# Sums of logarithms as two single-pass products of split parts, in a gated linear attention followed by a feed-forward network

## The chip, the cores and the metric

The kernel runs on one core of a Trainium2 chip. The metric is the device time of one execution in microseconds; the median of four runs of the kernel before is 568.94 us (568.49 to 570.35). Traces come from one further look at such an execution, the one of 568.91 us.

## What is computed

Attention first: for each of 4 batches and 8 heads a 48 x 48 state is decayed by alpha, step by step over 768 positions, and read by q. Its output, one row of 384 numbers for each of 3072 tokens, goes through a feed-forward network with 2048 hidden units.

```python
for t in range(S):                      # S = 768, alpha between 0.8 and 1
    state = alpha[:, :, t, :, None] * state + np.einsum('bhd,bhe->bhde', k[:, :, t], v[:, :, t])
    y[:, :, t] = np.einsum('bhd,bhde->bhe', q[:, :, t], state)
x = y.transpose(0, 2, 1, 3).reshape(B * S, H * D)     # 3072 x 384
h = np.maximum(x @ w_in, 0.0)                         # w_in 384 x 2048, stored as 64-bit floats
out = (h * h @ w_out).astype(np.float32)              # w_out 2048 x 384, likewise
```

## The kernel before

**Blocks.** The sequence is cut into 6 chunks of 128 positions; a block is one chunk of one batch, all heads, 24 blocks in all. Block n is chunk n // 4 of batch n % 4. Within a block the recurrence is solved with cumulated decays: the logarithm of alpha is summed over the positions from the block's start (a product with a triangle of ones), q is multiplied by the exponential of that sum and k by the exponential of its negative; then scores, masked, times v, plus q times the state that came in.

The steps of a block that matter here, with the lines of the profile:
- `ln` (243): ScalarE takes the logarithm of alpha's tile in place, 128 positions x 384 columns.
- `cs` (248): TensorE multiplies it with `causal`, the 128 x 128 triangle of ones, in fp32, into one PSUM bank.
- `eb`, `ei` (258, 262): ScalarE takes exp of the sums and of their negative into the tiles `b` and `inv`, of which there are two each.
- `mq`, `mk` (266): VectorE multiplies q and k by them.
- `bl`, `br` (279, 285): SP's DMAs copy the last row of `b` to DRAM and back, turned, into one of four small tiles `last`, by which the state is multiplied (450).
- `turn` (515) and its copies (523): q and k are transposed on TensorE and copied out by ScalarE.
- `scores` (404), `state_sums` (430), `masked` (414), `y` (380), `ev` (538): the rest, in functions `ga` and `gb` that handle two blocks at a time.

**Feed-forward.** Four blocks make a group of 512 tokens, six groups in all. Group 0 is multiplied plainly (621, 696). For groups 1 to 5 both matrix products are done with seven instead of eight half-size products, the sums and differences of halves being made by VectorE (`combine`, line 570): a stage of products with `w_in` (659, results combined on 672 to 679) and then a stage of 28 units with `w_out` (730; results combined on 748 to 766). One unit is four fp32 products of 192 columns.

**Order.** Nothing is scheduled by a tool: each engine runs its instructions in the order in which the program issues them. Attention for group g + 1 is laid between the units of group g's last stage. Every pair of blocks has a table `PLAN` of times in units at which its steps are issued, counted from the pair's start; `weave` issues a step before the first unit whose time has come. The pairs that start with blocks 8, 14, 18 and 22 start at time 0 of a stage, those of 10 and 12 at units 7 and 14 of the first such stage, those of 16 and 20 at unit 13.5 of theirs. The pair's first lines before the change:

```python
PLAN = (
    (0, "ln0"),
    (0.5, "ln1"),
    (2.0, "cs0 eb0 ei0"),
    (3.0, "cs1 eb1 ei1"),
    (3.5, "mk0"),
```

So in a stage the logarithms are issued before units 0 and 1, and the two products with the triangle before units 2 and 3. Each `cs` is followed on SP's queue by the load of alpha for the block after next, into the tile that is read by `cs`. Blocks 0 to 3 are issued from a list written by hand; blocks 4 to 7 are laid between the units of group 0.

Of the kernel before, what the change touches and what calls it, by code (L numbers as in the profile page):

```python
# [7 lines left out]

FP32 = mybir.dt.float32
U32 = mybir.dt.uint32  # L10
AF = mybir.ActivationFunctionType
ALU = mybir.AluOpType
# [3 lines left out]
GB = 4  # L16
# [7 lines left out]
def kernel(  # L24
# [25 lines left out]
    nc = tc.nc  # L50
    B, H, S, D = q.shape
    C = 128
    NCH = S // C
    NP = H // 2
# [8 lines left out]
    consts = ctx.enter_context(tc.tile_pool(name="consts", bufs=1))  # L63
# [3 lines left out]
    p2 = ctx.enter_context(tc.tile_pool(name="p2", bufs=2))  # L67
# [6 lines left out]
    def kept(name, n, shape):  # L74
        return [consts.tile(shape, FP32, name=f"{name}{i}") for i in range(n)]

    s_t = [p2.tile([128, NP, 64], FP32, tag="s", name="s", bufs=B + 2) for _ in range(B)]
    for t in s_t:
# [9 lines left out]
    NW = 8  # L88
    w_in = [consts.tile([128, KM, DF // NW], FP32, name=f"w_in{i}") for i in range(NW)]
    w_out = [consts.tile([128, NJ // NW, DM], FP32, name=f"w_out{i}") for i in range(NW)]  # L90
    HM, NR2 = DM // 2, NJ // 4
    tsum = [kept(f"t{i}_", NR2, [128, 2, HM]) for i in (1, 2, 4)]

    def flat(t):
        return t.rearrange("a x y -> a (x y)")
# [4 lines left out]
    for x, n, i in (("q", 2, 6), ("q", 3, 7), ("k", 3, 5)):  # L100
        t = lent[x, n] = flat(w_out[i])[:, 0 : 64 * H].rearrange("a (h d) -> a h d", h=H)
# [19 lines left out]
    def load_weights(i):  # L121
        dst = (w_in + w_out)[i]
        dt = moe_w_in.dtype
        raw = dst if dt == FP32 else raw_pool.tile(list(dst.shape), dt, tag="raw", name="raw")
        raws[i] = raw
# [13 lines left out]
    def convert_first(i):  # L139
        if moe_w_in.dtype == FP32:  # L140
            return
        w = (w_in + w_out)[i].rearrange("a k f -> a (k f)")
        n = w.shape[1]
        words = raws.pop(i).rearrange("a k f -> a (k f)").bitcast(U32)
        words = words.rearrange("a (n h) -> a n h", h=2)
        lo, hi = words[:, :, 0], words[:, :, 1]
        power = cv_pool.tile([128, n], U32, tag="power", name="power")
        upper = cv_pool.tile([128, n], U32, tag="upper", name="upper")
        nc.vector.tensor_scalar(
            out=power, in0=hi, scalar1=20, scalar2=0x7FF,  # L150
            op0=ALU.logical_shift_right, op1=ALU.bitwise_and,
        )
        nc.vector.tensor_scalar(
            out=upper, in0=hi, scalar1=0xFFFFF, scalar2=None, op0=ALU.bitwise_and
        )
        half[i] = w, lo, hi, power, upper
# [46 lines left out]
    make_identity(nc, ident)  # L203
    causal = consts.tile([128, C], FP32, name="causal")
    make_upper_triangular(nc, causal, 1.0, diag=True)
    halves_mask = consts.tile([128, C // 2], FP32, name="halves_mask")
    for i in range(2):
        rows = slice(64 * i, 64 * (i + 1))
        nc.gpsimd.tensor_copy(out=halves_mask[rows], in_=causal[rows, rows])
    last_t = kept("last", 4, [128, NP])  # L210
    for t in last_t:
        nc.gpsimd.memset(t, 0.0)
    dram = ctx.enter_context(tc.tile_pool(name="dram", bufs=1, space=bass.MemoryType.DRAM))
    rows_t = [dram.tile([1, H * D], FP32, name=f"row{n}") for n in range(NBLK)]
    rebias = consts.tile([128, 1], FP32, name="rebias")
# [13 lines left out]
    blk = [{} for _ in range(NBLK)]  # L229
    xT = {}  # L230

    def bank(n, name, shape=(NP, C)):

        if n < GB and name in ("sc", "y"):
            return ps_ffn.tile([128, *shape], FP32, tag="f", name=name)
        return ps_att.tile([128, *shape], FP32, tag="att", name=name)
# [4 lines left out]
    def ln(n):  # L241
        la = blk[n]["la"] = tile_of("a", n)
        nc.scalar.activation(out=la, in_=la, func=AF.Ln)

    def cs(n):

        ps = blk[n]["cs"] = bank(n, "cs")
        nc.tensor.matmul(  # L248
            out=ps.rearrange("a p t -> a (p t)")[:, 0 : H * D], lhsT=causal,
            rhs=blk[n].pop("la"), start=True, stop=True,  # L250
        )

    def sums_of_logs(n):
        return blk[n]["cs"].rearrange("a p t -> a (p t)")[:, 0 : H * D]
# [83 lines left out]
    def am(n):  # L338

        ps = blk[n].pop("sc")  # L340
        for e in range(2):
            nc.vector.copy_predicated(
                out=am_t[n % NAM][:, e],
                mask=causal.bitcast(U32).unsqueeze(1).to_broadcast([128, NP, C]), data=ps[e],
            )
# [63 lines left out]
    def masked(n):  # L409
# [3 lines left out]
        for e in range(2):  # L413
            nc.vector.copy_predicated(  # L414
                out=am_h(n)[:, e, n % 2], data=ps[e][:, 0],
                mask=halves_mask.bitcast(U32).unsqueeze(1).to_broadcast([128, NP, 64]),
            )

    def am_h(n):
        t = am_t[n // 2 % NAM].rearrange("a e p t -> a (e p t)")  # L420
        return t.rearrange("a (e m p t) -> a e m p t", e=2, m=2, p=NP)
# [351 lines left out]

    stages = [(ln, cs, eb, ei, mq, mk, bl, br), (qT, qc, kT, kc), (sc, am), (kv, y, ev, st)]
    steps = {f.__name__: f for stage in stages for f in stage}
    steps["load"] = load
    steps["weights"] = lambda _: load_weights(to_load.pop(0))
# [15 lines left out]
    for word in first.split():  # L795
# [6 lines left out]

    PLAN = (
        (0, "ln0"),
        (0.5, "ln1"),
        (2.0, "cs0 eb0 ei0"),
        (3.0, "cs1 eb1 ei1"),
        (3.5, "mk0"),
# [62 lines left out]
    for g in range(1, NG):  # L871
# [8 lines left out]
        if g + 1 < NG:  # L880
            n = GB * (g + 1) + 2
# [35 lines left out]
```

## Time and profile before

| what | value |
|---|---|
| median of 4 runs | 568.94 us |
| the profiled execution | 568.91 us, of which its span (first to last instruction) is 566.9 us |
| TensorE busy, multiplying | 553.7 us, 98% of the span |
| TensorE busy, loading weights (beside it) | 470.4 us, 83% |
| VectorE busy | 327.0 us, 58%, in 655 instructions |
| ScalarE busy | 223.7 us, 39% |
| GpSimd busy | 5.8 us, 1% |
| line 248, the product with the triangle | 48 instructions (two for each of 24 blocks), 486 to 590 ns each as recorded |
| granted TensorE clock | 1.000 over the span |

The profile lists instructions by engine: PE is TensorE's multiplying, PEld its loading of weights, DVE VectorE, ACT ScalarE, POOL GpSimd, SPq the queue from which SP issues DMAs. "L248" is line 248 of the kernel. Instructions on TensorE overlap, so that the length of one is more than what it adds to the stream; what it adds is seen from the start of one to the start of the next. In timeline rows the columns are the start in us, the length, the engine, the line, the operation, the tile written and the tiles read, the shapes, the count that was merged into the row and, in brackets, how long the engine had been idle and what ended that.

### The profile page before, as it was taken

Reading aid. Unit: us, or ns where it says so; the run is one execution under the profiler, and the core shown is the slowest. Engines: PE = TensorE matmul, PEld = TensorE weight load, DVE = VectorE, ACT = ScalarE, POOL = GpSimd, SP = SyncE. Lnnn points to the kernel's source line nnn. Section 1 sums busy time; section 2 is a strip of 40 time slices with the busy share of each in tenths; the row PEclk is TensorE's granted clock in tenths of the full one; section 3 lists DMA queues with packets and bytes.
Section 4 is the critical chain, followed back from the end, with each engine's and each line's share of the span. In section 5 each row is a group of like instructions: output and inputs, shape, how many; then the busy total and the mean of one; then the engine's idle time right before and its main releaser. Section 6 shows DMA issues by size and latency. Waiting matters only on the chain.

```text
span 566.9 us, 12556 instructions
## 1 busy us (share of the span) xinstructions
PE 553.7 (98%) x5306; PEld 470.4 (83%) x5306; DVE 327.0 (58%) x655; ACT 223.7 (39%) x533; POOL 5.8 (1%) x28
## 2 busy tenths in 40 slices
PE   8889999999999999999899999999999999999997
PEld 6654455668889899888899988999988999988996
DVE  4988688685874745565562566462466551466430
ACT  5469865442334353234143333433333340333100
POOL 2010000000000000000000000000000000000000
PEclk9999999999999999999999999999999999999999
DMA  9978576401003645000333200333300000100001
GB/s 164 254 177 217 152 183 209 114 1 57 1 1 57 114 98 103 28 0 16 57 72 77 65 1 1 57 59 71 86 0 2 0 3 1 57 0 2 1 0 57
DMA packets 117087, 37.04 MB, mean 65 GB/s; under 512 B 108820, under 2 KB 111912, under 8 KB 117032
## 3 DMA queue, kind: packets, MB, share of 16 engines
q1 hardware_dynamic: 117032, 36.25, 28.4%
q8 instruction: 42, 0.69, 0.5%
q14 instruction: 13, 0.11, 0.1%
HBM read 31.49 MB, written 4.75 MB: 64 GB/s over the span
## 4 chain that ended last, share of the span: by engine, by line
PE 95%; DMA 2%; DVE 2%; issue 1%; SPq 0%; ACT 0%; DVEq 0%
PE h L659 34%; PE o L730 33%; PE o L696 7%; PE h L621 7%; PE y L380 4%; PE cs L248 3%; PE T L515 2%; PE sckv L404 2%; PE sckv L430 2%; DMA raw<-in_moe_w_in_dram 1%; DMA k_in<-in_k_dram 1%; PE sc L333 0%; DVE xT L538 0%; PE qT L291 0%; PE kv L350 0%
## 5 line engine op out<-in xcount | busy, mean ns | idle before, releaser
L659 PE MATMUL h<-xT,w_in 128*128 128x256 f32 x480 | 124.0, 379 | 0.0
L659 PEld LDWEIGHTS h<-xT,w_in 128*128 128x128 f32 x480 | 91.1, 190 | 12.4
L730 PEld LDWEIGHTS o<-w_out,hid 128*128 128x128 f32 x480 | 79.1, 190 | 4.1
L730 PE MATMUL o<-w_out,hid 128*128 128x192 f32 x480 | 82.5, 326 | 0.0
L538 ACT COPY xT<-y 32x256 f32<-32x256 f32 (+2 forms) x132 | 46.1, 364 | 63.5 <-PE y L380 60.0
L672 DVE TENSOR_TENSOR hid<-h,u 128x256 f32<-128x256 f32 x120 | 50.9, 424 | 28.8 <-PE h L659 25.0
L677 ACT ACTIVATE hid<-hid 128x256 f32<-128x256 f32 x40 | 16.7, 417 | 114.6 <-DVE hid L672 114.6
L672 DVE TENSOR_TENSOR u<-h,u 128x256 f32<-128x256 f32 x80 | 33.9, 423 | 34.8 <-PE h L659 22.4
L659 PE MATMUL h<-s3x,ws 128*128 128x256 f32 x160 | 47.6, 379 | 0.0
L621 PE MATMUL h<-xT,w_in 128*128 128x512 f32 (+1 forms) x108 | 43.5, 550 | 3.3 <-ACT xT L538 1.8
L414 DVE COPY_PREDICATED am<-halves_mask,sckv 128x256 f32<-128x256 uint32 x40 | 15.5, 442 | 52.9 <-PE sckv L430 52.9
L696 PE MATMUL o<-w_out,hid 128*128 128x384 f32 x128 | 42.8, 490 | 0.0
L730 PE MATMUL o<-t,s 128*128 128x192 f32 x240 | 41.8, 327 | 0.0
L659 PE MATMUL h<-s3x,w_in 128*128 128x256 f32 x160 | 41.1, 379 | 0.0
L730 PEld LDWEIGHTS o<-t,s 128*128 128x128 f32 x240 | 39.3, 190 | 0.7
L621 PEld LDWEIGHTS h<-xT,w_in 128*128 128x128 f32 x108 | 20.0, 190 | 23.4 <-issue 16.3
L696 PEld LDWEIGHTS o<-w_out,hid 128*128 128x128 f32 x128 | 23.9, 190 | 16.2 <-issue 0.2
L659 PEld LDWEIGHTS h<-s3x,w_in 128*128 128x128 f32 x160 | 30.4, 190 | 4.1
L659 PEld LDWEIGHTS h<-s3x,ws 128*128 128x128 f32 x160 | 30.4, 190 | 4.1
L730 PE MATMUL o<-t,hid 128*128 128x192 f32 x160 | 28.1, 330 | 0.0
L679 DVE SCALAR_TENSOR_TENSOR hid<-hid 128x512 f32<-128x512 f32 x40 | 27.3, 681 | 0.0
L764 DVE TENSOR_TENSOR osb<-o,us 128x384 f32<-128x384 f32 x10 | 5.6, 558 | 37.0 <-PE o L730 37.0
(120 smaller groups left out, 750.6 us busy)
## 6 DMA issues: line engine op xcount, KB each, us to landing
raw<-in_moe_w_in_dram SPq DMA_DIRECT2D x8, 768.0 KB
raw<-in_moe_w_out_dram SPq DMA_DIRECT2D x8, 768.0 KB, 4.9
v_in<-in_v_dram SPq DMA_DIRECT2D x24, 192.0 KB, 3.7
out_dram<-osb SPq DMA_DIRECT2D x24, 192.0 KB, 1.9
k_in<-in_k_dram SPq DMA_DIRECT2D x23, 192.0 KB, 4.2
a_in<-in_alpha_dram SPq DMA_DIRECT2D x22, 192.0 KB, 2.6
q_in<-in_q_dram SPq DMA_DIRECT2D x22, 192.0 KB, 3.5
last<-row SPq DMA_DIRECT2D x40, 0.8 KB, 3.1
```

Of the source, the lines that this page charges most:

```text
L248: nc.tensor.matmul(out=ps.rearrange("a p t -> a (p t)")[:, 0 : H * D], lhsT=causal, rhs=blk[n].pop("la"), start=True, stop=True,)
L380: ins = nc.tensor.matmul(out=ys[e][64 * half : 64 * half + D + G * e, m % 2, p // 2, t], lhsT=lhsT, rhs=rhs, start=(half, e) not in seen, ...
L404: nc.tensor.matmul(out=ps[e][HALF[h], 0, p, :], lhsT=ks[rows, p, HALF[h]], rhs=qs[rows, p, HALF[h]], start=True, stop=True, skip_group_che ...
L414: nc.vector.copy_predicated(out=am_h(n)[:, e, n % 2], data=ps[e][:, 0], mask=halves_mask.bitcast(U32).unsqueeze(1).to_broadcast([128, NP, ...
L538: copy(out=x[to : to + m, kk, t : t + 2], in_=blk[n]["y"][e][r : r + m, :, p // 2],)
L621: nc.tensor.matmul(out=ps, lhsT=w[:, kk, c0 : c0 + 128], rhs=xT[g][:, kk, cols], start=(kk == 0), stop=(kk == KM - 1),)
L659: nc.tensor.matmul(out=ps, lhsT=a, rhs=b, start=(step.isupper() and i == 0), stop=(i == len(pairs) - 1), skip_group_check=True,)
L672: nc.vector.tensor_tensor(out=o, in0=ps, in1=z, op=ALU.add)
L677: nc.scalar.activation(out=h1[:, HT : 2 * HT], in_=h1[:, HT : 2 * HT], func=AF.Relu)
L679: nc.vector.scalar_tensor_tensor(out=h2, in0=h2, scalar=0.0, in1=h2, op0=ALU.max, op1=ALU.mult)
L696: nc.tensor.matmul(out=acc[t][:, 0:DM], lhsT=hid[i][:, j, t * C : (t + 1) * C], rhs=w_out[i][:, j, :], start=(i == 0 and j == 0), stop=(i ...
L730: nc.tensor.matmul(out=acc[k][:, t, :], lhsT=lhs[:, j, t * C : (t + 1) * C], rhs=rhs[:, j, :], start=(first and r + j + t == 0), stop=(r = ...
```

## The change

From block 8 on the logarithms are split by VectorE into two parts, each short enough for a 4-byte format of which TensorE makes a single pass (`float32r`): `hi` is the logarithm rounded to that format, `lo` the rest. Both are multiplied with a copy of the triangle in that format, one after the other into the same bank. Blocks 0 to 7 keep the fp32 product.

The new step `sp` stands between `ln` and `cs`: at 0.5 units for the first block of a pair and at 1.0 for the second. `hi` and `lo` take their buffers from the two each of `b` and `inv`. The load of alpha's tile for the block after next has now to wait for `lo`, which is alpha's last reader. Apart from that the four tiles `last` become slices of one, cleared by one instruction of GpSimd instead of four, and GpSimd makes the triangle's copy at the start.

```diff
+    causal_r = consts.tile([128, C], FP32R, name="causal_r")
+    nc.gpsimd.tensor_copy(out=causal_r, in_=causal)
...
-    last_t = kept("last", 4, [128, NP])
-    for t in last_t:
-        nc.gpsimd.memset(t, 0.0)
+    last = consts.tile([128, 4, NP], FP32, name="last")
+    nc.gpsimd.memset(last, 0.0)
+    last_t = [last[:, i, :] for i in range(4)]
...
+    SPLIT = 2 * GB
+
+    def sp(n):
+        if n < SPLIT:
+            return
+        la = blk[n].pop("la")
+        hi = p2.tile([128, H * D], FP32R, tag="b", name="hi")
+        lo = p2.tile([128, H * D], FP32R, tag="inv", name="lo")
+        nc.vector.tensor_copy(out=hi, in_=la)
+        nc.vector.tensor_tensor(out=lo, in0=la, in1=hi.bitcast(FP32), op=ALU.subtract)
+        blk[n]["parts"] = hi, lo
+
     def cs(n):
         ps = blk[n]["cs"] = bank(n, "cs")
-        nc.tensor.matmul(
-            out=ps.rearrange("a p t -> a (p t)")[:, 0 : H * D], lhsT=causal,
-            rhs=blk[n].pop("la"), start=True, stop=True,
-        )
+        out = ps.rearrange("a p t -> a (p t)")[:, 0 : H * D]
+        if n < SPLIT:
+            nc.tensor.matmul(out=out, lhsT=causal, rhs=blk[n].pop("la"), start=True, stop=True)
+            return
+        hi, lo = blk[n].pop("parts")
+        nc.tensor.matmul(out=out, lhsT=causal_r, rhs=hi, start=True, stop=False)
+        nc.tensor.matmul(out=out, lhsT=causal_r, rhs=lo, start=False, stop=True)
...
     PLAN = (
         (0, "ln0"),
-        (0.5, "ln1"),
+        (0.5, "ln1 sp0"),
+        (1.0, "sp1"),
         (2.0, "cs0 eb0 ei0"),
```

## The prediction

> **What bounds the kernel now.** I read the page's chain that ended last first, then the timeline around every product on line 248 from block 8 on, then single durations.
>
> ```profile
> PE 95%; DMA 2%; DVE 2%; issue 1%; SPq 0%; ACT 0%; DVEq 0%
> ```
>
> Nothing but TensorE is worth naming on the path; the second table agrees (PE 9 in every slice from the fourth but the last, granted clock 9 throughout). So a microsecond taken from or added to TensorE's stream after the start is a microsecond of the span, and VectorE, ScalarE and the queues count only where TensorE waits for them. The product to be changed, in the timeline of the first feed-forward stage that carries a pair (blocks 8 and 9):
>
> ```profile
> 170.26 0.92 ACT L243 ACTIVATE a_in<-a_in 128x384 f32<-128x384 f32 x2
> 170.38 0.69 DVE L570 TENSOR_TENSOR s3x<-hid 128x512 f32<-128x512 f32 x1 [0.55 <-ACT hid L678]
> ...
> 171.21 0.81 PE L248 MATMUL cs<-a_in,causal 128*128 128x384 f32 x2
> ...
> 171.86 1.46 PE L730 MATMUL o<-w_out,hid 128*128 128x192 f32 x8
> ...
> 173.16 0.81 PE L248 MATMUL cs<-a_in,causal 128*128 128x384 f32 x2
> ```
>
> Columns: start, length, then engine, line and tiles. One fp32 product is two instructions, each with its own weight load. From start to start it holds TensorE 171.86 - 171.21 = 0.645 us, 0.3225 per instruction; the eight 192-column ones behind it take 173.16 - 171.86 = 1.30, or 0.1625 each. Both are 0.84 ns a column, and the loads vanish under them. And the logarithm (ACT, line 243) is done only 0.44 us before TensorE comes to line 248.
>
> **What the change takes away.** 16 blocks (8 to 23) lose 0.645 us each and get two single passes of 384 columns. No row shows such a pass. The nearest row, line 248's own instruction, gives 0.3225 as the upper end (nothing gained). For the lower end: that product splits its weights over two loads; if each instruction also streams the moving operand twice, a pass is half of 0.3225, 0.161, and with the 192-column instruction as the same amount of work 0.1625. I take 0.1625, because two loads for one product show that fp32 is handled in two parts, and nothing in the rows is cheaper. A pair of passes is then 0.325 and a block saves 0.32 us: 16 x 0.32 = 5.1 us, if nothing waits. The Trainium skill ("FP8 and Floating Point Precision", TensorE Precision Notes) counts four passes through the array for true fp32 and names a reduced form that reads four bytes and truncates; no run here shows that form, and one pass of the four would be the same 0.161.
>
> **What it adds.** Two VectorE instructions a block, hi (a copy) and lo (a subtraction), between the logarithm and the product. Durations:
>
> ```profile
> L266 DVE TENSOR_TENSOR k_in<-k_in,inv 128x384 f32<-128x384 f32 x23 | 12.7, 554 | 13.4 <-ACT inv L262 10.2 <-DMA k_in<-in_k_dram 3.2
> ...
> L149 DVE TENSOR_SCALAR power<-raw 128x768 uint32<-128x768 uint32 x16 | 8.9, 555 | 3.1 <-DMA raw<-in_moe_w_out_dram 2.6 <-DMA raw<-in_moe_w_in_dram 0.4
> ```
>
> lo has two inputs of 384 columns, like line 266: 0.55. For hi the bounds are 0.55 (same width, two inputs) and what line 149 gives: one input, 768 columns in the time of 384. By these two rows the fixed part is about 0.155 and a one-input column costs 0.52 ns, so 0.355. I take 0.355, the one-input row. The skill ("VectorE: DVE Perf Modes", the section on the TRN2 errata) tabulates 58 cycles plus columns over the speed-up for such a copy, 0.26 us; line 149's 0.555 contradicts that table (0.46), so the row decides; by the table the sum below would be 0.6 us lower.
>
> A dependent instruction starts 0.03 behind its predecessor's end (lines 449 and 450: 0.42 long, 187.32 to 187.78); an independent one of 384 columns 0.465 after its predecessor's start (192.90, 193.36, 193.83). From the start S of hi, lo ends at S + 0.355 + 0.03 + 0.55 = S + 0.93, and the second block's lo at S + 1.79. What TensorE pays when it must wait is in the start-up:
>
> ```profile
> 11.36 0.52 ACT L243 ACTIVATE t<-t 128x384 f32<-128x384 f32 x1 [0.21 <-DMA t<-in_alpha_dram]
> ...
> 11.94 0.30 PEld L248 LDWEIGHTS cs<-t,causal 128*128 128x128 f32 x2 [0.17 <-ACT t L243]
> 11.94 0.91 PE L248 MATMUL cs<-t,causal 128*128 128x384 f32 x2
> ```
>
> 0.06 us after the producer's end the weight load starts, not hidden now: the pair is 0.91 instead of 0.81, so 0.10 for the load. The pass over lo then takes 0.1625. TensorE goes on at S + 0.93 + 0.06 + 0.10 + 0.16 = S + 1.25.
>
> **Now each pair.** Every pair's first product is the doubtful one; its second is a unit or more later and always finds its lo ready.
>
> Blocks 8, 14, 18, 22 (at the head of a stage, all four with the gaps above): hi stands behind line 570 on VectorE, which frees it 0.61 after its start (as 181.85 to 182.46), at 170.99; the logarithm ended at 170.77. S = 170.99, TensorE goes on at 172.24 instead of 171.86: **0.38 us lost** each, where 0.32 was to be won. Four times: +1.52.
>
> Block 10, from the next pair's timeline:
>
> ```profile
> 181.85 0.69 DVE L570 TENSOR_TENSOR s3x<-s3x,hid 128x512 f32<-128x512 f32 x1 [1.94 <-PE o L730]
> 181.96 1.01 ACT L243 ACTIVATE a_in<-a_in 128x384 f32<-128x384 f32 x2
> 182.46 1.29 DVE L570 TENSOR_TENSOR hid<-hid 128x512 f32<-128x512 f32 x2
> 182.79 0.35 PEld L248 LDWEIGHTS cs<-a_in,causal 128*128 128x128 f32 x2
> 182.95 0.81 PE L248 MATMUL cs<-a_in,causal 128*128 128x384 f32 x2
> 183.28 1.49 PEld L730 LDWEIGHTS o<-t,s 128*128 128x128 f32 x8
> 183.59 1.46 PE L730 MATMUL o<-t,s 128*128 128x192 f32 x8
> ```
>
> ScalarE comes late to the logarithm here (copies of the pair before); the first takes 0.61, so S = 182.60 and TensorE goes on at 183.85, not 183.59: +0.26. Block 12 is the same with 196.33 for the logarithm and 198.18 for TensorE: 198.22, +0.04.
>
> Blocks 16 and 20 lie late in their stage:
>
> ```profile
> 289.20 1.89 DVE L570 TENSOR_TENSOR s<-hid,s 128x512 f32<-128x512 f32 x3
> 289.63 0.94 ACT L243 ACTIVATE a_in<-a_in 128x384 f32<-128x384 f32 x2
> ...
> 292.67 0.81 PE L248 MATMUL cs<-a_in,causal 128*128 128x384 f32 x2
> ```
>
> In the changed program hi stands behind two of the three (0.60 each, S = 290.40); lo ends at 291.33, 1.3 us early. Block 20's gaps are the same (378.15, 378.58, 381.63). These two and all eight second blocks keep their 0.32: ten times, -3.20.
>
> Sum: 1.52 + 0.26 + 0.04 - 3.20 = **-1.4 us** of the profiled execution's 568.91 (span 566.9, 2.0 around it, untouched; the median, 568.94, is the same to 0.03). **567.5 us.**
>
> **What costs nothing, and its cover.** The 32 VectorE instructions add 13 us of occupancy to an engine that idles 1 to 3 us around each pair. Behind the splits stand line 570's subtractions (blocks 10, 11: they end near 185.4; the masks behind them wait for scores until 186.20), a sum and two stores (12, 13: end near 200.4, masks at 200.78) and the same (16, 20). If the copy took 0.55, those of block 12 would be 0.1 late, and their results are read units later. lo releases alpha's tile for SP's reload, earlier than the product did. hi and lo borrow buffers of exp and its inverse, whose last readers (line 266, the row's DMA) finished a pair earlier. Set-up gives GpSimd one more small copy and three fewer fills; nothing there is late.
>
> **Rivals.**
> 1. *The copy runs at one column per cycle* (0.55): six exposed firsts, 0.2 each, +1.2: 568.7. Against: line 149.
> 2. *Slower: a pass isn't half.* Place: TensorE at line 248. Ten blocks pay it twice, six once (the first pass hides in the wait): 26 passes. At 0.3225: 26 x 0.16 = +4.2, so 571.7. The change loses from 0.1625 + 1.4/26 = 0.216 us a pass on. For: no row of a pass under 0.84 ns a column. Against: the two loads.
> 3. *Weights of the other format aren't loaded under the running product*: 0.10 on entry and exit of each of eight unexposed blocks, 0.10 once for the other eight: +2.4: 569.9. The switch to the 48-row tiles shows 0.23 us of "issue" idle of this kind (before lines 404 and 515), but those change the array's rows, which this doesn't.
> 4. *The wait is smaller*: lo's weights are loaded before its wait (6 x 0.10), and the copy's fixed part is only that of VectorE's one-column fill on line 216, 0.06, so that it is 0.26 long (6 x 0.095): 566.4 with both. Against: line 248's load at 11.94 came behind the wait, and line 149's fixed part.
>
> **The numbers.** Forecast 0.50, rival 1 0.10, rival 2 0.16, rival 3 0.10, rival 4 0.14. 0.3% of 568.94, about what a measurement can tell from no change, is 1.7 us: the forecast lies just inside, at -0.25%. Its own scatter (0.1 us at each of six waits, and TensorE's single 1.5 us "issue" gap at 281.2, which may go or come again in the changed stream) puts some two fifths of it beyond 1.7. Faster: 0.20 + 0.14 = 0.34; slower: 0.16, and 0.07 for rivals 1 and 3 together or another such gap, 0.23; same 0.43. The range runs from rival 4, 566.3, to rival 2, 571.8.
>
> **To be seen in the profile after.** Passes of line 248's successor 0.16 apart and the unit behind blocks 9, 11, 13, 15 to 17 and so on starting 0.325 after them; a copy of 0.355 and a subtraction of 0.55 per block; TensorE idle about 0.7 us in front of hi and lo together at blocks 8, 14, 18, 22, less at 10 and 12, not at all at 16 and 20. A pass of 0.32, a load outside its cover, or line 570's results arriving late at TensorE would prove me wrong.

## The result and the profile after

The changed kernel takes 568.55 us in the median (53 runs), the kernel before, run beside it, 568.97 us (79 runs). The ratio of the mean times is 0.9987, with a 95% interval of 0.9981 to 0.9994: -0.7 us (-0.3 to -1.1); the two medians alone differ by 0.42, which lies in it too. That is a small gain, half of what was forecast.

The profiled execution of the changed kernel is itself one of the longer ones (570.36 us, span 568.4), so its total is not to be set beside that of before. Its windows say why. The columns are: stretch in us, its length, busy time of PE, PEld, DVE, ACT and POOL with counts, granted TensorE clock, DMA share, GB/s:

```profile
35.10:38.50 3.40, 3.40 (x10) 2.69 (x10) 3.34 (x5) 0.80 (x3) 0.00 (x0) 0.50 0.96 302
280.00:284.30 4.30, 2.79 (x154) 2.59 (x144) 2.54 (x6) 0.00 (x0) 0.00 (x0) 1.00 0.25 50
284.30:287.70 3.40, 3.40 (x59) 2.96 (x61) 0.00 (x0) 0.16 (x1) 0.00 (x0) 0.50 0.02 5
```

Twice the clock was halved for 3.4 us, each time after TensorE had idled; the execution of before that was profiled had no such window. So what the change does must be read from gaps in the timeline, not from the two spans.

The first pair of a stage (blocks 8 and 9), in the timeline of the changed kernel; line 246 is the logarithm, 258 hi, 259 lo, 270 and 271 the passes over them, 750 the unit's products:

```profile
171.15 0.92 ACT L246 ACTIVATE a_in<-a_in 128x384 f32<-128x384 f32 x2
171.28 0.69 DVE L590 TENSOR_TENSOR s3x<-hid 128x512 f32<-128x512 f32 x1 [0.55 <-ACT hid L698]
171.89 0.35 DVE L258 CAST hi<-a_in 128x384 fp32r<-128x384 f32 x1
172.28 0.56 DVE L259 TENSOR_TENSOR lo<-a_in,hi 128x384 fp32r<-128x384 f32 x1
172.29 0.19 PEld L270 LDWEIGHTS cs<-hi,causal_r 128*128 128x128 f32 x1 [0.32 <-DVE hi L258]
172.30 0.44 PE L270 MATMUL cs<-hi,causal_r 128*128 128x384 f32 x1
172.75 0.35 DVE L258 CAST hi<-a_in 128x384 fp32r<-128x384 f32 x1
172.89 0.19 PEld L271 LDWEIGHTS cs<-lo,causal_r 128*128 128x128 f32 x1 [0.41 <-DVE lo L259]
...
173.17 1.46 PE L750 MATMUL o<-w_out,hid 128*128 128x192 f32 x8
...
174.34 0.48 PE L270 MATMUL cs<-hi,causal_r 128*128 128x384 f32 x1
174.47 0.19 PEld L271 LDWEIGHTS cs<-lo,causal_r 128*128 128x128 f32 x1
174.65 0.34 PE L271 MATMUL cs<-lo,causal_r 128*128 128x384 f32 x1
174.65 1.34 PEld L750 LDWEIGHTS o<-w_out,hid 128*128 128x128 f32 x8
174.82 1.46 PE L750 MATMUL o<-w_out,hid 128*128 128x192 f32 x8
```

Read it in two halves. Above, the unit in front had begun at 170.81 and would have let TensorE go on at 172.11. TensorE stands still for hi and again for lo (the brackets behind PEld), and the next unit starts at 173.17. Below, block 9: its lo was ready at 173.70, nothing is waited for, and the stream runs through. Block 16, late in its stage, goes through like block 9:

```profile
292.84 0.35 DVE L258 CAST hi<-a_in 128x384 fp32r<-128x384 f32 x1
293.23 0.56 DVE L259 TENSOR_TENSOR lo<-a_in,hi 128x384 fp32r<-128x384 f32 x1
...
294.97 0.47 PE L270 MATMUL cs<-hi,causal_r 128*128 128x384 f32 x1
...
295.29 0.34 PE L271 MATMUL cs<-lo,causal_r 128*128 128x384 f32 x1
```

And the list of who waited for whom, for TensorE's loads (us in total, times, longest):

```profile
PEld cs L271 <- DVE lo L259: 2.3, 6, 0.4
PEld cs L270 <- DVE hi L258: 1.3, 4, 0.3
```

Six waits for lo, four of them with one for hi ahead: the six first products that were named. From the page, the line that answers to the chain shown of before:

```profile
PE 62%; DVE 1%; ACT 1%; issue 1%
```

The shares do not reach 100%, because this chain could be followed back only to block 12's split, near 197 us. Inside it TensorE still carries nearly everything, and of VectorE hi and lo have come in (0.3% and 0.4% of the span).

For each product, the time on TensorE from the start of the last product ahead of it to the start of the first behind it (so 0.16 us of it is the product ahead), in us. The product ahead is taken in because the record of a pass over hi begins early, at block 9 0.03 us behind the start of that product; so the passes are seen 0.31 us apart and the unit 0.17 behind the second, not 0.16 and 0.16.

| blocks | before | after | difference each | foreseen |
|---|---|---|---|---|
| 8, 14, 18, 22 | 0.81 | 1.22 to 1.23 | +0.415 | +0.38 |
| 10 | 0.81 | 1.10 | +0.29 | +0.26 |
| 12 | 0.81 | 0.885 | +0.08 | +0.04 |
| 9, 15, 16, 17, 19, 20, 21, 23 | 0.81 | 0.515 | -0.29 | -0.32 |
| 11, 13 (behind a change of tiles) | 0.90 | 0.61 | -0.29 | -0.32 |

The sum is 1.66 + 0.29 + 0.08 - 2.92 = -0.9 us, inside the measured interval.

### The profile page after: what moved, and what is told of

Read it like the earlier page. It is cut to its first block, busy times and chain, and to the rows that moved or that the text cites. A ratio compares the mean times of both kernels' runs of the same rounds, so it can differ in the third digit from the quotient of the medians.

```text
span 568.4 us, 12584 instructions
## 1 busy us (share of the span) xinstructions
PE 554.9 (98%) x5306; PEld 472.4 (83%) x5306; DVE 339.9 (60%) x687; ACT 223.7 (39%) x533; POOL 5.9 (1%) x26
## 4 chain that ended last, share of the span: by engine, by line
PE 62%; DVE 1%; ACT 1%; issue 1%
PE o L750 28%; PE h L679 27%; PE y L400 3%; PE sckv L424 1%; PE T L535 1%; PE sckv L450 1%; PE cs L271 1%; DVE lo L259 0%; ACT hid L698 0%; PE cs L270 0%; DVE hi L258 0%; DVE hid L692 0%; ACT hid L697 0%; DVE osb L784 0%; ACT qs L543 0%
## 5 line engine op out<-in xcount | busy, mean ns | idle before, releaser
L641 PE MATMUL h<-xT,w_in 128*128 128x512 f32 (+1 forms) x108 | 45.0, 567 | 2.6 <-ACT xT L558 1.8
```

The source lines that it names most:

```text
L641: nc.tensor.matmul(out=ps, lhsT=w[:, kk, c0 : c0 + 128], rhs=xT[g][:, kk, cols], start=(kk == 0), stop=(kk == KM - 1),)
```

## The experiments

Theory 1: a block whose lo is ready saves 0.29 us, six first products wait, and nothing else matters. Its rivals, numbered for this section alone: 1, the small edits (the slices of one tile, the triangle's copy) carry the difference; 2, VectorE's extra work holds something up; 3, the loss goes with the format or the split itself, not with the wait; 4, a wait that is taken away comes back elsewhere. Differences are against the kernel before, run beside each, and follow from the ratio and its interval.

**The rest of the change alone.**

```diff
-    SPLIT = 2 * GB
+    SPLIT = NBLK
```

> The rest of the change alone: every block keeps the fp32 product and no split is made; the four tiles of the last rows are slices of one and the triangle's copy is made at the start. Theory 1 (the gain comes from the passes, the loss from the wait for lo): 0.0 us against before, within 0.3. Rival (the small edits carry the difference): the whole -0.7 us.

Measured: ratio 0.9994 (0.9982 to 1.0007), -0.3 us (-1.0 to +0.4). No difference is seen; that the whole -0.7 comes from here isn't excluded by these times alone. In its trace, though, all 16 products take 0.81 or 0.90 as before, and the four stages of the last table are as long as before to 0.02 us, with TensorE no earlier at the first of them (169.2 us, 168.6 before); so rival 1 falls.

**The splits made, and not used.** Both parts are computed and left unused; the product takes the logarithm.

```diff
-        la = blk[n].pop("la")
+        la = blk[n]["la"]
...
+        nc.tensor.matmul(out=out, lhsT=causal, rhs=blk[n].pop("la"), start=True, stop=True)
```

> hi and lo are made by VectorE as in the change, but the product stays one fp32 product of the logarithm itself, so no engine waits for the split (the parts are left unused). Theory 1: VectorE's 32 instructions (13 us busy) stand beside TensorE and cost nothing: 0.0 us against before, 0.3 at most. Rival 2 (they hold up line 590's sums, the masks or the stores, for which TensorE then waits): 0.5 to 2 us slower than before.

Measured: 1.0004 (0.9994 to 1.0014), +0.2 us (-0.3 to +0.8). In its trace all 16 products take 0.81 or 0.90, as before. VectorE's busy time is 13 us longer and costs nothing that can be seen: by its time rival 2 falls for its upper three quarters, and its four stages (56.07, 52.47, 50.53, 46.00) are none of them longer than before, which leaves nothing of it.

**hi alone.** lo is neither made nor multiplied, so the sums lose the logarithms' low bits.

```diff
-        nc.vector.tensor_tensor(out=lo, in0=la, in1=hi.bitcast(FP32), op=ALU.subtract)
...
-        nc.tensor.matmul(out=out, lhsT=causal_r, rhs=hi, start=True, stop=False)
-        nc.tensor.matmul(out=out, lhsT=causal_r, rhs=lo, start=False, stop=True)
+        nc.tensor.matmul(out=out, lhsT=causal_r, rhs=hi, start=True, stop=True)
```

> lo is neither made nor multiplied, one pass of hi a block (the sums lose the low bits of the logarithms). Theory 1, from after's rows: a pass is 0.16 us, so a block with no wait holds TensorE 0.35 instead of 0.81 with the unit's last product included (ten times -0.46); the first blocks of the four pairs at a stage's head go on 0.65 us after the last product instead of 0.81 (-0.16 each), block 10 -0.22, block 12 -0.44: together -5.9 us, about 563.0. If a pass were 0.32, or the wait were for hi as much as for lo, under half of that.

Measured: 0.9880 (0.9867 to 0.9893), -6.8 us (-6.1 to -7.6). Its trace has 0.335 to 0.34 per block without a wait (0.35 foreseen), 0.63 at the heads of stages (0.65), 0.57 for block 10; these sum to -6.1. So a pass costs 0.34 - 0.1625 = 0.175 us and lo costs a waiting block another 0.6 (1.22 - 0.63): more than three times what it costs one that doesn't wait (0.515 - 0.34 = 0.175).

**Both products a unit later**, for every pair from block 8 on.

```diff
+                    if n0 >= SPLIT:
+                        w += {"cs0": 1.0, "eb0": 1.0, "ei0": 1.0, "cs1": 1.0, "eb1": 1.0, "ei1": 1.0,
+                              "mk0": 1.0, "bl0": 0.5, "mq0": 0.5, "mk1": 0.5, "bl1": 0.5}.get(f, 0)
```

> From block 8 on the two products of a pair and what follows them stand one unit (1.3 us) later in the table, the splits where they are. Theory 1: no product waits any more and all 16 blocks keep the 0.29 us that a block without a wait saves: -4.7 us against before, 564.3, that is -3.8 against the change. Rival 3 (the time is lost to something that goes along with the split, such as a switch of formats): as the change, -0.7. Rival 4 (the wait moves on: exponentials and line 286 come late for the transposes on line 535): some 2 us of it given back there.

Measured: 0.9999 (0.9987 to 1.0010), 0.0 us (-0.7 to +0.6). The total is rival 3's or 4's. The trace says where: 14 of the 16 blocks take 0.51 to 0.52 (0.60 for 10 and 11), as theory 1 has it, and block 13 takes 3.77. Its timeline:

```profile
203.23 4.34 ACT L558 COPY xT<-y 32x256 f32<-32x256 f32 x12 [1.02 <-PE y L400]
...
206.84 0.29 PEld L270 LDWEIGHTS cs<-hi,causal_r 128*128 128x128 f32 x1 [2.88 <-ACT xT L558]
```

A unit later it is issued behind the 12 copies that empty the outputs of the pair before, and its bank is one that these copies give free. 14 times 0.29 won, 2.87 lost at block 13 and 0.17 at block 12: -1.0. The rest is the clock, which was halved behind that wait: the stage is 59.34 us long where its blocks' terms give 58.3, so the window takes back 1.1 more.

```profile
203.00:206.70 3.70, 1.10 (x76) 0.96 (x66) 2.46 (x7) 3.35 (x10) 0.00 (x0) 1.00 0.67 131
206.70:210.10 3.40, 3.25 (x10) 3.26 (x11) 1.44 (x3) 1.70 (x5) 0.00 (x0) 0.50 0.47 95
```

Eleven of its 12 runs show a mean clock of 0.993 to 0.997; the one at 1.000 took 567.87 us, 1.3 us under the median of those 17 runs of before beside it that had 0.998 or more (569.15); that is a single run, but it fits. Rival 4 is right, but for one block and at another place than I had named (a bank, not the transposes).

**The same without block 13:** the pairs that start with 8, 10, 14, 18 and 22 alone.

```diff
-                    if n0 >= SPLIT:
+                    if n0 >= SPLIT and t < 10:
```

> As the run with both products a unit later, but for the pairs that start with blocks 8, 10, 14, 18 and 22 alone; those of 12, 16 and 20 keep the change's times, so that block 13's product isn't put behind the copies on line 558. Theory 1: the waits of 8, 14, 18, 22 (0.42 each) and 10 (0.29) go and these blocks save 0.29 too; only block 12's 0.08 is left: by the rows -4.3 us against before. Rival 3 (the loss belongs to the format or to VectorE, not to the wait): -0.7. Rival 4 (the wait moves on to the transposes): between -0.7 and -2.5.

Measured: 0.9931 (0.9919 to 0.9943), -3.9 us (-3.3 to -4.6); median 565.44. Fifteen blocks take 0.51 to 0.52 or 0.60. Of the waits for lo, one is left:

```profile
PEld cs L271 <- DVE lo L259: 0.3, 1, 0.3
```

It is block 12's, which holds TensorE longer than in the change (1.15 against 0.885); that TensorE comes to it sooner, because block 10's wait ahead is gone, fits, but was not tried. In sum -15 x 0.29 + 0.34 = -4.0. Theory 1 holds, rival 3 falls. This is the fastest of the kernels here that compute the whole.

**The splits earlier instead:** for the four pairs at a stage's head the logarithms and splits are issued ahead of the last step of the stage before.

```diff
+            n0 = GB * (g + 1) + (0 if g == 1 else 2)
+            if j == NJ // 2 and n0 < NBLK:
+                early.update((n0, n0 + 1))
+                for f in (ln, sp):
+                    for n in (n0, n0 + 1):
+                        f(n)
             for i, step in enumerate("ABacCDd"):
...
+                        if f[:-1] in ("ln", "sp") and n in early:
+                            continue
```

> The logarithms and splits of the four pairs at a stage's head (8, 14, 18, 22) are issued before the last step of the stage ahead, the products stay where the change has them. Theory 1: these four waits go, block 10's 0.29 and block 12's 0.08 stay: -3.7 us against before. Rival 4b: the splits now stand ahead of lines 692 and 699 on VectorE and hold up the last hidden rows; as these are first used three units into the next stage, theory 1 expects nothing of it, the rival 1 us a stage, that is as the change or slower.

Measured: 0.9951 (0.9935 to 0.9968), -2.8 us (-1.8 to -3.7), just reaching what was expected. The same kernel again:

> The same kernel as the run with early splits, to see whether its total comes to what its stages show. Theory 1: -3.7 us against before, as the traced stages add up to; rival 4b (early splits cost 1 us a stage somewhere that the stages don't show): -2.8 or less again.

Measured: 0.9939 (0.9926 to 0.9952), -3.5 us (-2.7 to -4.2). In the trace of the first of the two, the stage ahead is 37.99 us long, to the hundredth as before, so rival 4b's late hidden rows don't exist; the heads' products take 0.51, and the four stages are together 3.7 us shorter than before, as expected. This trace also has a window of halved clock at 35 us, as the changed kernel's has. In the second trace the products are the same, but the four stages are only 2.7 us shorter: TensorE pauses there for 0.74 us at 219.2 (0.32 before) and for 0.51 us at 371.6 (the last section tells of such pauses). So what the two runs fell short of is of the size that pauses and clock make; run by run it isn't settled.

**Both ways together:** early splits, and block 10's pair a unit later.

```diff
+                    if n0 >= SPLIT and 5 < t < 10:
+                        w += {"cs0": 1.0, "eb0": 1.0, "ei0": 1.0, ...
```

> The early splits of the run above, and for block 10's pair alone the products a unit later: only block 12 waits. Theory 1: -4.3 us against before, as the run with five pairs later, since both take the same waits away in two ways.

Measured: 0.9941 (0.9925 to 0.9957), -3.4 us (-2.4 to -4.3): as the run with five pairs later within the intervals, the expected value at the edge.

**Only the ten blocks that had no wait.**

```diff
-    SPLIT = 2 * GB
+    PARTED = {9, 11, 13, 15, 16, 17, 19, 20, 21, 23}
...
-        if n < SPLIT:
+        if n not in PARTED:
```

> The change for the ten blocks alone that had no wait (9, 11, 13, 15, 16, 17, 19, 20, 21, 23); the six first blocks keep the fp32 product. Theory 1: ten times 0.29, -2.9 us against before, four times the change's gain with fewer blocks changed. If the gain did not come from the passes of these ten, or the loss not from the six, it stays near the change's -0.7.

Measured: 0.9954 (0.9942 to 0.9966), -2.6 us (-1.9 to -3.3). The ten take 0.51 to 0.52 or 0.60, the six 0.81. Fewer blocks changed, and clearly more won: the six first blocks together lose in the change.

**The split from block 4 on**, together with the five pairs later. By the same condition the pair of blocks 4 and 5 is set later too.

```diff
-    SPLIT = 2 * GB
+    SPLIT = GB
```

> As the run with five pairs later, and the split begins with block 4: blocks 4 to 7 too get two passes, while group 0's weights are being converted on VectorE, three of whose instructions are 0.95 us long each (lines 172 to 179). Theory 1, if lo is ready there: four more times 0.29, -1.2 us beyond that run, -5.2 against before. If the rule is that the first product waits wherever VectorE's queue ahead of the split is longer than the two units or so of lead, blocks 4 to 7 lose more than they save: -2 to -4 against before.

Measured: 1.0010 (0.9997 to 1.0023), +0.6 us (-0.2 to +1.3). That is 4 to 5 us worse than the same without blocks 4 to 7, more than I had allowed for, and in its trace, which is 2.7 us longer, it comes from a wait of another kind:

```profile
73.21 0.36 DVE L258 CAST hi<-a_in 128x384 fp32r<-128x384 f32 x1 [5.07 <-ACT a_in L246]
...
73.67 0.56 DVE L259 TENSOR_TENSOR lo<-a_in,hi 128x384 fp32r<-128x384 f32 x1
...
74.15 0.95 DVE L172 SCALAR_TENSOR_TENSOR power<-raw,power 128x768 uint32<-128x768 uint32 x1
...
76.00 0.96 DVE L179 TENSOR_TENSOR w_in<-w_in,power 128x768 f32<-128x768 f32 x1
...
77.02 0.30 PEld L641 LDWEIGHTS h<-xT,w_in 128*128 128x128 f32 x2 [2.17 <-DVE w_in L179]
```

VectorE stood 5.07 us in front of hi, which waited for the logarithm, and the conversion of weights stood behind it in the queue. TensorE then waited 2.17 us, not for lo, but for those weights. Its multiplying waited for them four times, 4.3 us in all, against once and 0.6 us in the run with five pairs later. The rest of the distance between the medians the trace doesn't show; eleven of the twelve runs have a mean clock of 0.991 to 0.997, and of the run with five pairs later none is under 0.998.

The stages in which the changed blocks lie, from their first product to the next stage's first, in us (the changed kernel's second one contains a window of halved clock):

| kernel | blocks 8 to 13 | 14 to 17 | 18 to 21 | 22, 23 |
|---|---|---|---|---|
| before | 56.40 | 52.74 | 50.53 | 46.00 |
| the change | 56.27 | 53.58 | 50.28 | 46.12 |
| five pairs later | 55.15 | 51.49 | 49.49 | 45.41 |
| splits early | 55.49 | 51.69 | 49.35 | 45.41 |
| ten blocks alone | 55.87 | 51.14 | 50.08 | 45.70 |

The last column is the change in small: one head and one second block, +0.42 - 0.29 = +0.12, and with the wait gone twice -0.29.

## Why the prediction was right, and where it was off

The time lies in the range, which says little, since that is 5.5 us wide and holds gain and loss; but the sign is right, and the mechanism is the one that was forecast, product by product. The amount is half: -0.7 measured, -1.4 forecast. Going through the steps:

- *A pass of 0.1625, a pair 0.325, 0.32 saved.* Nearly: the pass is about half of the fp32 instruction, as the two loads of one product had suggested, but a pair holds TensorE 0.515 - 0.1625 = 0.35 us, and a pass alone 0.175. Ten blocks without a wait therefore save 2.9 instead of 3.2. This is the first mis-sized term, 0.3 us. The second rival (a pass of 0.32) is out.
- *hi 0.355, lo 0.55, 0.03 between them.* Measured 0.35, 0.56 and 0.04. The copy does take the 0.53 ns a column of the one-input row of line 149 (0.555 - 0.35 us over 384 columns more); rival 1 is out. The two rows named in the prediction leave the fixed part open, though; it takes a third, line 570's 0.69 us for 512 columns of two inputs, to come to 0.15. The table of the Trainium skill ("VectorE: DVE Perf Modes", the section on the TRN2 errata), which comes to 0.26 for such a copy by estimate, is too low here too.
- *S, and TensorE going on at S + 1.25.* S came out as worked out (0.22 ahead of the slot at block 8, 171.89 against 172.11), and TensorE goes on at S + 1.28. The heads lose 0.415 instead of 0.38, block 10 0.29 instead of 0.26, block 12 0.08 instead of 0.04: the second term, 0.2 us in all. Both terms together bring the forecast's -1.4 to the -0.9 of the table. Rival 4 is out as well: lo's weight load starts behind its wait (172.89, lo ends at 172.84), and the copy is 0.35, not 0.26.
- *Blocks 16 and 20 and all second blocks don't wait.* Right for all ten, and the run with these ten alone has the gain by itself.
- *The other work of VectorE costs nothing.* Right (the splits made and not used), where VectorE has gaps; the run from block 4 on shows the price where it hasn't.
- *Rival 3, loads not hidden at a change of format, 0.10 each way.* The timeline of block 9 shows lo's load under hi's pass and the next unit's under lo's. What a pair takes above 0.325 is 0.03, a seventh of this rival's 0.2.
- *The single 1.5 us gap at 281.2 may go or come.* It came again, at 282.09. Whether the clock is halved behind it differs from run to run; this widens what single executions show by more than the change is worth.

## What to carry to other kernels

An edit that makes a product cheaper by handing its operand to another engine is worth (saving) x (blocks whose operand is early) - (wait) x (blocks whose operand is late); work out both counts from the timeline, pair by pair, before adding up savings. Here the wait at six blocks took back 2.0 of 2.9 us, and moving five pairs' products by one unit, where no bank and no queue stood in the way, made -0.7 us into -3.9. A split that waits in an in-order queue also holds everything behind it, so it belongs where its own input has long been there.

## What the runs showed of the hardware

From 210 us on TensorE's longest gap stands at the same place of its instruction stream in all twelve traces (the kernel before, the change and the ten runs): behind 5313 instructions, counting loads, products and those of its sequencer, between 1.2 and 1.8 us from start to start, at 278 to 284 us. Its rows in the changed kernel:

```profile
281.52 0.57 PE L400 MATMUL y<-am,v_in 64*48 64x64 f32 x23
...
283.59 0.21 PEld L400 LDWEIGHTS y<-am,v_in 64*48 64x48 f32 x8 [1.65 <-issue]
283.60 0.34 PE L400 MATMUL y<-am,v_in 64*48 64x64 f32 x8 [1.51 <-issue]
```

In the kernel with hi alone the instruction behind the gap is another (a product of a unit), so the gap belongs to the place in the stream and not to what is computed there. It lies in the stretch of smallest products (23 in 0.57 us above). The record shows more of this kind: from 84 us on the twelve traces hold 24 shorter pauses, 0.28 to 0.76 us, between products on less than the full 128 rows and columns, and all stand behind 1473, 3521, 4289, 6081, 6337 or 7361 instructions (one is off by a single instruction), each a multiple of 256 away from 5313. Which of these places show a pause differs from run to run. The Trainium skill ("Runtime: NRT & Kernel Launch", Instruction fetch mechanics) says that instructions are fetched in blocks of 256 and that this is mostly hidden. That such a fetch is the cause here fits the distances of 256, but was not tried.

The clock is halved for one window of 3.4 us after some idle times of TensorE and not after others of the same length: behind the gap above in the changed kernel's profile and not in that of before (1.7 us both), and behind the 2.9 us wait of block 13 in the trace of that run, eleven of whose twelve runs have a mean clock to match. What a window cost can be read from the stages: 1.1 us behind block 13, and 1.3 us here (53.58 us, where the stage of before and the products' terms give 52.3). By estimate 3.4 us at half clock lose at most half, 1.7. Each is more than this change brings.
